# Seven of sixteen head pairs transposed by VectorE, nine by TensorE in place, the last queries of two pairs scored together, and the order of all instructions written out

## The chip, the cores and the metric

The kernel runs on one core of one Trainium2 chip. The core has TensorE for matrix products, VectorE, ScalarE and GpSimd for work on elements, and SyncE, whose queue issues the DMAs. TensorE writes to PSUM, eight banks of 512 float32 columns on 128 partitions; everything else lies in SBUF or, behind the DMAs, in HBM. The metric is the time of one execution in microseconds, the median of the runs shown. In the profile TensorE's products stand as PE, its weight loads as PEld, VectorE as DVE, ScalarE as ACT, GpSimd as POOL.

## What is computed

```python
B, H, S, D = 4, 8, 576, 64
q_rot, k_rot = rotate(q), rotate(k)          # x1*cos - x2*sin, x1*sin + x2*cos
scores = matmul(q_rot, k_rot^T) / sqrt(D)
attn = exp(scores - max(scores))
attn = attn / (sum(attn) + 1e-9)
x = (attn @ v), heads side by side           # 4 x 576 tokens of 512
xn = (x - mean) / sqrt(var + 1e-6) * g_ln
out = x + relu(xn @ w_ch1) @ w_ch2           # 512 -> 2048 -> 512
```

All of it is float32 in and out. The MLP's weights come as 64-bit words that the kernel decodes itself, and each is split into a high and a low part in TensorE's float32r format, so that one product takes three passes (high x high, high x low, low x high).

## The kernel before

The 32 heads are worked in 16 pairs (index i); a pair's two heads j share the 128 partitions, 64 each. `attention(i)` goes over the 576 queries in five groups c: four of 128 queries, each giving two units (one per head) of 128 queries by 576 keys, and a last group of 64 queries, in which both heads fill one unit. A unit lies in two PSUM banks. `scores` (L425, products in L432 and L436) writes it; VectorE takes the maximum of each row (L477); ScalarE takes the exponential and the sum (L489). The result p has queries on the partitions, while the product with v needs keys there, so TensorE transposes p, 128 x 128 at a time (L533), with smaller steps for the tail of the keys (L553) and for the last queries (L572, L573), into PSUM, and VectorE or ScalarE copies it out (`copy`, L285). The product with v is made in two parts of 256 and 320 queries: one product over the keys left over (L621) and sixteen records over the others (L625), two heads side by side in 64 columns each. The sums get an epsilon (L499, L501), are inverted (L505), transposed by TensorE to a row (L591), copied, written to memory and read back spread over the partitions, and the scaling (L635) writes x.

Before that, `prepare(i)` loads queries and keys and turns them by the rotary angles: three elementwise steps each for keys and queries, 6 a pair, 90 for pairs 1 to 15 (L403, L405), on GpSimd but for pair 1, where VectorE may take them.

Beside attention run `decode` and `weight_sums`: every weight tile is put together from its bits by ScalarE, VectorE and GpSimd (L765 to L794), stored to memory, and combined into sums of quarters (L840 to L850) that the second stage uses. The tokens lie in five blocks. `layer_norm(n)` normalizes one: means by a TensorE product (L669), squares by ScalarE (L698), their mean by four groups of products in 32 columns each (L685), and the spread of the inverse (L714). Block 0 goes through the MLP beside attention (`mlp_unit`, L889, 32 units of twelve products). Blocks 1 to 4 go in two pairs (`pair_inputs`, `pair_stage`, L1042), each pair by a scheme with seven products in place of eight: 2 pairs x 8 stages x 7 units of twelve products.

The order of all work comes from `Plan.run`. Every step is a task with the engines that it may run on and an assumed duration on each, what it comes after, which buffers of which ring it takes and gives back (`RINGS`), and a priority. The planner goes through time, starts the first task that can start, on the engine that is free first, and records it; the instructions of each engine are then chained in that order. `reorder` shifts the priorities by drawn amounts (`ORDER`). Score units take slots of two banks ("sc", three); transpositions and products with v take single banks ("t", two). After the first layer norm the third score slot becomes two single banks ("m"), which the MLP and the layer norms use.

```python
tt = add({"PE": 0.47}, tr, [exps[2 * c + j]], N + 0.1 * j, take=[ring_t(i, j)], ...)
...
parts[a].append(add(how_c, cp_, deps, N + 0.1 * j, take=take, give=[ring_t(i, j)], ...))
...
how2 = {"POOL": 1.43, "DVE": 0.76} if i < 2 else {"POOL": 1.43}
```

Of the kernel before, what the change touches and what calls it, by code (L numbers as in the profile page):

```python
# [10 lines left out]
F32 = mybir.dt.float32  # L11
# [9 lines left out]
P = 128  # L21
S = 576
# [14 lines left out]
PARTS = slice(0, 2 * P), slice(2 * P, S)  # L37
# [17 lines left out]
TM = 99  # L55
RATE = 285.0
EARLY = 30.0
AFTER = 0.0
SLACK = 0.7
XPRIO = 1e4  # L60
XB = 0.0
WARM = 16
HOLD = {28: (14, 2), 29: (15, 0), 30: (15, 2), 31: (15, 4)}
ORDERED = True
ORDER = [
# [5 lines left out]
]  # L71
SIZES = 0.5, 2.0, 5.0, 12.0, 30.0
SHARE = 0.08, 0.01, 0.1, 0.3, 0.3
# [4 lines left out]
def mixed(x):  # L78
    for m in (0x7FEB352D, 0x846CA68B):
        x = ((x ^ x >> (16 if m == 0x7FEB352D else 15)) * m) & 0xFFFFFFFF  # L80
    return x ^ x >> 16


def chance(seed, i):
    return mixed((mixed(seed) + i * 0x9E3779B9) & 0xFFFFFFFF) / 2.0**32


def reorder(tasks):
    kinds = {}
    kind = [kinds.setdefault(t.fn.__code__, len(kinds)) for t in tasks]  # L90
    n = len(tasks)
    for seed in ORDER:
        m = mixed(seed)
        size, mode, later = SIZES[m % 5], m // 5 % 5, m // 25 % 5 == 0
        lo = int(chance(seed, 7) * n) if mode == 3 else 0
        for i in range(lo, min(lo + 60, n) if mode == 3 else n):
            t = tasks[i]
            if later and "SP" not in t.how:
                continue
            k = kind[i] + 1000003 if mode in (0, 4) else i  # L100
            if chance(seed, 2 * k + 100) < SHARE[mode]:
                d = size * (2 * chance(seed, 2 * k + 101) - 1)
                if later:
                    t.release += d
                else:
                    t.prio += d


class Task:
    def __init__(self, how, fn, after, prio, take, give, lag, release, name, behind, port, over, of, which):  # L110
# [3 lines left out]
        self.start = self.end = None  # L114


class Plan:
# [32 lines left out]
    def run(self):  # L150
        free = dict.fromkeys(("PE", "DVE", "ACT", "POOL", "SP", "NONE"), 0.0)
        slots = {k: [(0.0, j) for j in range(n)] for k, n in RINGS.items()}
        channel = port = 0.0
        reorder(self.tasks)
        waiting = sorted(self.tasks, key=lambda t: t.prio)
        now = 0.0
        while waiting:
            later = []
            started = False
            for t in waiting:  # L160
                at = t.release
                for a in t.after:
                    if a.end is None:
                        at = None
                        break
                    at = max(at, a.end + (0.0 if t.how.keys() == {a.engine} != {"SP"} else a.lag))
                if at is None or any(a.start is None for a in t.behind):
                    continue
                picked = []
                for k, r in enumerate(t.take):  # L170
                    fit = [x for x in slots[r] if t.which is None or x[1] == t.which][t.take[:k].count(r) :][:1]
                    if not fit:
                        at = None
                        break
# [1091 lines left out]
```

## Time and profile before

| | us |
|---|---|
| median of three runs | 693.29 |
| lowest, highest | 692.33, 695.5 |
| span of the profiled execution, first to last instruction | 690.1 |
| PE busy | 670.6 |
| DVE busy | 515.5 |
| POOL busy | 417.3 |
| ACT busy | 376.0 |

For the profiled execution only its span is recorded; the median of the runs lies 3.2 us above it. Busy times count overlapping records once. Matmuls overlap in the array, so the duration of one record is longer than the distance to the next; the distance is read from the chain of waits, where a group of records stands with the time by which it moved the chain on.

### The profile page before, as it was taken

What the parts mean: (1) busy time and instruction counts of PE and PEld (TensorE: products, weight loads), DVE (VectorE), ACT (ScalarE), POOL (GpSimd) and SP (SyncE); (2) the same over time, 40 slices, a digit from 0 to 9 for tenths busy, and PEclk for the clock granted to TensorE, in tenths of its full rate; (3) what the DMA queues carried; (4) which work ended last, traced back from release to release, by engine and by line L of the source; (5) the groups of instructions that cost most, each with busy time, mean ns of one, the idle gap of its engine ahead of it and who ended that gap; (6) DMA issues with size and microseconds to landing.
All of it is one profiled execution on the core that took longest, in us unless ns stands there. A gap on an engine that the chain in (4) does not pass through costs nothing.

```text
span 690.1 us, 11545 instructions
## 1 busy us (share of the span) xinstructions
PE 670.6 (97%) x3954; PEld 506.5 (73%) x3954; DVE 515.5 (75%) x856; ACT 376.0 (54%) x805; POOL 417.3 (60%) x318
## 2 busy tenths in 40 slices
PE   6889999999999999999999999999999999999997
PEld 5555555667656667666666669989999999999996
DVE  4789888778877777778776759885877768757574
ACT  2678779667669676687666644341434243414130
POOL 4668866657769498787793614761457727515153
PEclk8899999999999999999999999999999999999999
DMA  8455664455947766568575347759678886666663
GB/s 270 138 175 179 238 215 158 152 180 168 318 164 249 249 236 217 194 228 302 193 245 191 118 153 242 219 186 307 213 214 262 270 269 206 221 217 214 211 217 133
DMA packets 85323, 147.20 MB, mean 213 GB/s; under 512 B 10880, under 2 KB 56592, under 8 KB 85264
## 3 DMA queue, kind: packets, MB, share of 16 engines
q1 hardware_dynamic: 84128, 145.60, 64.2%
q10 hardware_dynamic: 1136, 0.85, 0.4%
q8 instruction: 32, 0.52, 0.3%
q14 instruction: 27, 0.22, 0.1%
HBM read 108.60 MB, written 37.82 MB: 212 GB/s over the span
## 4 chain that ended last, share of the span: by engine, by line
PE 88%; ACT 5%; DVE 4%; DMA 1%; issue 1%; ACTq 0%; DVEq 0%
PE n L1042 40%; PE m L889 12%; PE sc L436 10%; PE t L625 9%; PE t L533 8%; PE sc L432 2%; PE t L621 2%; PE t L572 1%; ACT p L489 1%; PE t L553 1%; ACT pt L285 1%; DVE mx L477 1%; PE m L685 1%; DVE ws L850 1%; PE t L591 1%
## 5 line engine op out<-in xcount | busy, mean ns | idle before, releaser
L1042 PE MATMUL n<-x,w 128*128 128x448 f32 x672 | 140.1, 367 | 0.0
L1042 PEld LDWEIGHTS n<-x,w 128*128 128x128 f32 x672 | 125.5, 188 | 12.2 <-issue 1.1
L477 DVE TENSOR_REDUCE mx<-sc 128x1 f32<-128x576 f32 x144 | 104.5, 749 | 31.9 <-PE sc L436 24.7
L489 ACT ACTIVATE p<-sc,mx 128x576 f32<-128x576 f32 x144 | 106.0, 740 | 28.6 <-DVE mx L477 24.0
L1042 PE MATMUL n<-o,w 128*128 128x448 f32 x576 | 121.0, 368 | 0.0
L1042 PEld LDWEIGHTS n<-o,w 128*128 128x128 f32 x576 | 107.8, 188 | 10.9 <-issue 0.5
L969 ACT ACTIVATE o<-tmp 128x448 fp32r<-128x448 f32 x96 | 55.2, 579 | 104.8 <-PE n L1042 39.0
L976 POOL TENSOR_TENSOR o<-tmp,o 128x448 fp32r<-128x448 f32 x53 | 66.2, 1268 | 44.0 <-ACT o L969 43.2
L436 PE MATMUL sc<-xk,xq 64*128 64x288 f32 x512 | 85.2, 438 | 2.8 <-DVE xq L345 1.5
L533 PE MATMUL t<-ident,p 128*128 128x128 f32 x512 | 78.3, 285 | 7.0 <-DVE pt L285 1.9
L533 PEld LDWEIGHTS t<-ident,p 128*128 128x128 f32 x512 | 57.0, 143 | 37.9 <-issue 12.6
L285 ACT COPY pt<-t 128x512 f32<-128x512 f32 (+1 forms) x99 | 54.3, 551 | 53.8 <-PE t L533 46.6
L774 POOL TENSOR_TENSOR fw<-fw,w 128x512 int32<-128x512 int32 x32 | 43.3, 1358 | 44.0 <-ACT w L768 20.3
L625 PE MATMUL t<-pt,v 128*64 128x320 f32 (+1 forms) x512 | 69.1, 412 | 0.0
L436 PEld LDWEIGHTS sc<-xk,xq 64*128 64x128 f32 x512 | 48.2, 190 | 23.9 <-issue 10.8
L1114 DVE TENSOR_TENSOR xt<-xt,n 128x448 f32<-128x448 f32 x80 | 48.6, 615 | 18.9 <-PE n L1042 18.6
L625 PEld LDWEIGHTS t<-pt,v 128*64 128x64 f32 x512 | 33.9, 136 | 31.3 <-issue 12.3
L889 PE MATMUL m<-xh,w 128*128 128x512 f32 x128 | 47.9, 417 | 0.0
L889 PE MATMUL m<-hh,w 128*128 128x512 f32 x128 | 47.6, 415 | 0.0
L1101 POOL TENSOR_TENSOR tmp<-tmp 128x448 f32<-128x448 f32 x15 | 20.3, 1356 | 44.9 <-DVE tmp L1080 39.7
L405 POOL TENSOR_TENSOR xs<-xs,rope_sb 128x576 f32<-128x576 f32 x30 | 45.5, 1522 | 1.1 <-DMA xs<-in_qk 1.1
L285 DVE COPY pt<-t 128x512 f32<-128x512 f32 (+1 forms) x61 | 37.0, 613 | 10.2 <-PE t L533 6.6
(119 smaller groups left out, 1146.4 us busy)
## 6 DMA issues: line engine op xcount, KB each, us to landing
w<-s SPq DMA_DIRECT2D x64, 512.0 KB
w<-v SPq DMA_DIRECT2D x96, 256.0 KB
s<-ws SPq DMA_DIRECT2D x32, 512.0 KB
xs<-in_qk SPq DMA_DIRECT2D x30, 288.0 KB
w<-in_w1p SPq DMA_DIRECT2D x16, 512.0 KB
v<-w SPq DMA_DIRECT2D x16, 512.0 KB
w<-in_w2p SPq DMA_DIRECT2D x16, 512.0 KB
v<-in_vp SPq DMA_DIRECT2D x16, 320.0 KB
```

The costliest lines, as they stand in the source:

```text
L285: (ACT.copy if plan.engine == "ACT" else DVE.tensor_copy)(o, i)
L405: eng().tensor_tensor(out=x[step], in0=x[step], in1=rope_sb[:, step], op=ALU.mult)
L436: PE.matmul(ps[:, a, :HS], lhsT=q[r, c * P : (c + 1) * P], rhs=k[r, KEYS[a]], start=True, stop=True)
L477: DVE.tensor_reduce(out=mx, in_=st["ps", i, n][:, :, :HS], axis=AX.XY, op=ALU.max, negate=True)
L489: ACT.activation(out=halves(p), in_=st.pop(("ps", i, n))[:, :, :HS], func=AF.Exp, bias=st.pop(("mx", i, n)), scale=1.0, accum_out=total)
L533: PE.transpose(ps[:, k], p[:, j, j * T + k * P : j * T + (k + 1) * P], ident)
L625: PE.matmul(ps[r], lhsT=v[:, k, r], rhs=pt[:, j, k], start=False, stop=k == 3)
L889: PE.matmul(ps, lhsT=wt, rhs=x, start=c + m == 0, stop=c + m == NC + 1)
L969: ACT.activation(out=o[0], in_=x(), func=AF.Relu if relu else AF.Copy)
L976: eng().tensor_tensor(out=lo, in0=x(), in1=raw(hi), op=ALU.subtract)
L1042: PE.matmul(ps, lhsT=wt, rhs=x, start=fresh and kc + z == 0, stop=kc + z == 3, skip_group_check=True)
L1114: DVE.tensor_tensor(out=o, in0=o, in1=ps(which, h), op=ALU.add)
```

## The change

Of the 16 pairs, seven (4, 6, 8, 10, 12, 13, 15; those not in `TURNED`) have their exponentials transposed by VectorE, in place, in blocks of 32 x 32 (`turn`). Their product with v then runs over blocks of 32 keys: v lies in four shifted copies on the four groups of 32 partitions (four loads instead of one), and `pv` issues 18 x 4 x 2 products with 32 rows, 64 columns and 128 or 160 moving columns into four banks. The nine others are transposed by TensorE as before, but ScalarE alone copies the result back over the exponentials (`cross`, `back`), and their product takes all 576 queries at once, as 512 and 64 columns (`pv_crossed`).

The last 64 queries of pairs i and i + 1 (i even) are scored in one step of eight products (`tail_scores`), one tile for each pair. The sums of a pair lie in one tile; ScalarE adds the epsilon, VectorE inverts and transposes them, and they go through memory once a pair. In `layer_norm` of blocks 1 to 4 the four squares are added up by GpSimd or VectorE (`merge`), and TensorE takes one group of products instead of four. All PSUM is four slots of two banks, used by everything. The sums of the last two of eight weight groups are put off into the second stage (`late_sums`); the decoded weights go through memory for that. In `pair_inputs` the loads and steps are put in another order. The rings change: w from 6 to 4, v, inv and ws from 2 to 1, sq from 1 to 3. Every rotation step may now run on VectorE.

`reorder` no longer shifts priorities: a table of two characters a task (`PLACES`) gives each task its place, another (`SIDES`) its engine, 0 for the first named and 1 for the second, and `Plan.run` takes each engine's tasks in just that order.

```diff
-RINGS = {"sc": 3, "t": 2, "m": 2, "p": 3, "p9": 1, "pt0": 1, "pt1": 1, "x": 2, "xs": 3, "v": 2, "inv": 2, "w64": 2, "fw": 2, "w": 6, "h": 4, "xn": 1, "ln": 1, "sq": 1, "xt": 5, "n": 0, "o": 0, "tmp": 0, "ws": 2}
+RINGS = {"sc": 4, "m": 0, "pt": 2, "x": 2, "xs": 3, "v": 1, "inv": 1, "w64": 2, "fw": 2, "w": 4, "h": 4, "xn": 1, "ln": 1, "sq": 3, "xt": 5, "n": 0, "o": 0, "tmp": 0, "ws": 1, "lf": 0, "ls": 0}
-LATE = {"n": 6, "o": 13, "tmp": 9}
+LATE = {"n": 6, "o": 13, "tmp": 9, "lf": 1, "ls": 1}
+DEFERRED = 6
...
+TURNED = (0, 1, 2, 3, 5, 7, 9, 11, 14)
+ROPES = 16
+SUMMED = (1, 2, 3, 4)
...
+PLACES = (
...
+SIDES = (
...
+    places = "".join(PLACES)
+    for t, hi, lo in zip(tasks, places[::2], places[1::2], strict=True):
+        t.prio = len(CODE) * CODE.index(hi) + CODE.index(lo)
+    for t, side in zip(tasks, "".join(SIDES), strict=True):
+        t.side = list(t.how)[int(side)]
...
-            ld = add({"SP": 576 / RATE}, load, [], p - 8, behind=[ev["l_q"]], take=["x" + nm, "xs"], name=f"load{i}{nm}")
+            ld = add({"SP": 576 / RATE}, load, [], p - 8, behind=[ev["loaded"]] + ([ev["s", (i - 2, 4 - i % 2)]] if i > 1 else []), take=["x" + nm, "xs"], name=f"load{i}{nm}")
+            ev["loaded"] = ld
...
+            if i in TURNED:
+                SP.dma_start(v[:, 0], vp[divmod(i, NPB)].rearrange("p n d -> p (n d)"))
+                return
+            src = vp[divmod(i, NPB)].rearrange("(a k) n d -> k a (n d)", a=4)
+            for a in range(4):
+                SP.dma_start(v[a * BLK : (a + 1) * BLK], src)
+
+        ev["v", i] = add({"SP": 1.0 if i in TURNED else 6.2}, load, [], nominal(i, 0) - 4, behind=[ev["l_q"]], take=["v"], name=f"v{i}")
...
+    def tail_of(i, j):
+        d = j ^ i & 1
+        return slice(d * T, (d + 1) * T)
+
+    def tail_scores(i, tiles):
+
+        for a in range(2):
+            for j in range(2):
+                for n, ps in enumerate(tiles):
+                    k, q = st["k", i + n], st["q", i + n]
+                    r = slice(j * D, (j + 1) * D)
+                    PE.matmul(ps[tail_of(n, j), a, :HS], lhsT=q[r, S - T :], rhs=k[r, KEYS[a]], start=True, stop=True)
 
...
+        def turn(c):
+            p = st["pt", i][:, 4] if c == 4 else st["pt", i][:, c::5]
+            DVE.transpose(p, p)
...
+            two = st["turn", i, c] = banks[plan.task.got["sc"][0]]
+            p = flat()
+            if c < 4:
+                for j in range(2):
+                    for k in range(4):
+                        at = (2 * c + j) * S + j * T + k * P
+                        PE.transpose(two[:, j, k * P : (k + 1) * P], p[:, at : at + P], ident)
+                return
...
+        def invert():
+            t = totals[i % 2]
+            DVE.reciprocal(t[:, :9], t[:, :9])
+            st["row", i] = smp.tile([P, BLK], F32, name="row", bufs=2)
+            DVE.transpose(st["row", i], t)
...
+            if part == 0:
+                for go in both(slice(0, P), v[:, 0, 4 * P :], (S - T, S - T), True, False):
+                    go()
+            for k in ((0,), (1, 2), (3,))[part]:
+                halves_ = [both(slice(j * D, (j + 1) * D), v[:, 0, k * P + j * D :][:, :D], (j * (S + T) + k * P, (4 * j + k) * T), False, k == 3) for j in range(2)]
+                for pair in zip(*halves_):
+                    for go in pair:
+                        go()
...
+            for b in range(18 * part // PARTS, 18 * (part + 1) // PARTS):
+                for a in range(4):
+                    r = slice(a * BLK, (a + 1) * BLK)
+                    for j in range(2):
+                        k, of = divmod((b - 2 * j) % 18, 4)
+                        own = a // 2 == j ^ i & 1
+                        u0, u1 = (0, 4 + own) if j == 0 else (5 - own, 9)
+                        x0 = BLK if j == 0 or not own else 0
+                        if k == 4 and j:
+                            of += 2
+                        PE.matmul(
+                            tiles[a // 2][j * D : (j + 1) * D, a % 2, x0 : x0 + (u1 - u0) * BLK],
+                            lhsT=v[r, of, k * P + j * D : k * P + (j + 1) * D],
+                            rhs=pt[r, u0:u1, b * BLK : (b + 1) * BLK], start=b == 0, stop=b == 17)
...
+        def merge(c):
+            eng().tensor_tensor(out=z["sq", 0], in0=z["sq", 0], in1=z["sq", c], op=ALU.add)
...
+            if summed and c:
+                s = add(two, lambda c=c: merge(c), [s, v], N + 0.1 * c, give=["sq"], port=True)
+            if not summed or c == NC - 1:
+                v = add({"PE": 0.43}, lambda c=c: variance(c), [s], N, behind=[v] if c and not summed else [], give=["sq"], lag=0.2)
+            else:
+                v = s
...
+        if b < DEFERRED:
+            read, ev["sums", (y, g)] = make_sums(y, g, lambda: st["fw", b].bitcast(F32), l, prio, wsp, "ws", {"POOL": 1.3, "DVE": 0.68})
+            add({"NONE": 0.0}, lambda: None, read, prio, give=["fw"])
+            return
+        t = add({"SP": 1024 / RATE}, lambda: SP.dma_start(whole_w[y, g], st["fw", b].bitcast(F32)), [ev["d2", k] for k in range(k0, k0 + NC)], prio)
+        add({"NONE": 0.0}, lambda: None, l + [t], prio, give=["fw"])
+        ev["whole", (y, g)] = t
```

## Rows read from the trace of the kernel before

**Rows 1.** Busy time by stretch: stretch, length, busy PE, PEld, DVE, ACT, POOL (records), clock, DMA share, GB/s.

```profile
11.80:404.30 392.50, 381.93 (x2489) 246.25 (x2490) 305.81 (x521) 277.49 (x628) 283.02 (x207) 0.99 0.61 207
404.30:690.10 285.80, 281.89 (x1427) 254.60 (x1425) 203.55 (x315) 96.15 (x173) 131.68 (x104) 1.00 0.70 221
```

**Rows 2.** The page's strips over 40 slices: granted TensorE clock in tenths, and DMA rate.

```profile
PEclk8899999999999999999999999999999999999999
...
GB/s 270 138 175 179 238 215 158 152 180 168 318 164 249 249 236 217 194 228 302 193 245 191 118 153 242 219 186 307 213 214 262 270 269 206 221 217 214 211 217 133
```

**Rows 3.** The chain of waits, 140 to 182 us: start, step, engine, tile, line, records.

```profile
142.06 0.20 PE t L591
142.26 1.17 PE sc L436 x8
143.43 1.02 PE t L533 x8
...
145.86 0.22 PE t L553 x2
...
149.67 0.43 PE t L621 x2
150.10 1.88 PE t L625 x16
...
153.58 1.12 PE sc L432 x8
...
160.11 0.51 PE t L572 x8
160.62 0.06 PE t L573
...
164.45 2.77 PE m L889 x12
...
172.45 0.54 PE t L621 x2
172.99 2.33 PE t L625 x16
```

**Rows 4.** The chain of waits, 400 to 470 us.

```profile
406.77 0.33 PE m L685 x8
...
416.20 0.88 PE m L714 x8
417.08 29.27 PE n L1042 x144
446.35 0.75 PE m L669 x2
```

**Rows 5.** Groups by form: line, engine, operation, shapes, count, busy, mean ns, idle before.

```profile
L405 POOL TENSOR_TENSOR xs<-xs,rope_sb 128x576 f32<-128x576 f32 x30 | 45.5, 1522 | 1.1 <-DMA xs<-in_qk 1.1
...
L432 PE MATMUL sc<-xk,xq 64*64 64x288 f32 x128 | 19.0, 415 | 0.1
...
L850 DVE TENSOR_TENSOR ws<-fw,ws 128x512 fp32r<-128x512 f32 x12 | 14.9, 1239 | 2.7 <-ACT ws L847 2.6
...
L692 DVE TENSOR_TENSOR xc<-xt,m 128x448 f32<-128x448 f32 x16 | 9.0, 615 | 1.5 <-PE m L669 1.4
...
L692 DVE TENSOR_TENSOR xc<-xt,m 128x512 f32<-128x512 f32 x4 | 2.5, 682 | 0.6 <-PE m L669 0.6
...
L405 DVE TENSOR_TENSOR xk<-xk,rope_sb 128x576 f32<-128x576 f32 x1 | 0.8, 829 | 0.4 <-DMA xk<-in_qk 0.4
```

**Rows 6.** Busy time of L285 (DVE, ACT), then of L501 (DVE), 11.8 to 404.3 us.

```profile
11.80:404.30 392.50, 50.36 (x108) 66.32 (x148) 0.99 0.61 207
...
11.80:404.30 392.50, 15.89 (x21) 0.99 0.61 207
```

**Rows 7.** VectorE's instructions in order of time, 176 to 200 us.

```profile
175.81 1.58 DVE L850 TENSOR_TENSOR ws<-fw,ws 128x512 fp32r<-128x512 f32 x1
...
179.25 0.68 DVE L840 TENSOR_TENSOR fw<-fw 128x512 f32<-128x512 f32 x1
```

More of the change, by code (lines that the diff above doesn't have):

```diff
@@ L74 @@
 OVER = {"PE": 0.0, "DVE": 0.08, "ACT": 0.1, "POOL": 0.045, "NONE": 0.0}
 PORT = {"DVE": 0.13, "POOL": 0.05}
[L78 to L85, printed above, removed]
-def reorder(tasks):
[L89 to L106, printed above, removed]
+CODE = "ABCDEFGHIJKLMNOPQRSTUVWXYZabcdefghijklmnopqrstuvwxyz0123456789!#$%&()*+,-./:;<=>?@[]^_{|}~"
@@ L214, in run @@
-        self.length = max(t.end for t in self.tasks)
+        queues, ready, followers, missing, earliest = {e: [] for e in engines}, [], {}, {}, {}
+        for t in sorted(self.tasks, key=lambda t: t.prio):
+            missing[t], earliest[t] = len(t.after) + len(t.behind), 0.0
+            for a in [*t.after, *t.behind]:
+                followers.setdefault(a, []).append(t)
+            if t.side != "NONE":
+                queues[t.side].append(t)
+        ready = [t for t in self.tasks if t.side == "NONE" and not missing[t]]
@@ new lines, in begin @@
+        def begin(t):
+            at, picked = earliest[t], []
+            for k, r in enumerate(t.take):
+                fit = [x for x in slots[r] if t.which is None or x[1] == t.which][t.take[:k].count(r) :][:1]
+                if not fit:
+                    return None
+                picked.append((r, fit[0]))
+                at = max(at, fit[0][0])
+            if t.side == "SP" and at > 0:
+                at += SLACK
+            if t.side != "NONE":
+                at = max(at, free[t.side], port if self.shared(t, t.side) else 0.0)
+            return at, picked
@@ new lines, in attention, with part @@
+        N = nominal(i, 8) + 5
+        crossed = i in TURNED
+        count = 3 if crossed else PARTS
+        slots = ["sc"] if crossed else ["sc", "sc"]
+        for k in range(count):
+            def part(k=k):
+                (pv_crossed if crossed else pv)(k)
+            first, end = k == 0, k == count - 1
+            t = add({"PE": (2.13, 2.13, 1.1)[k] if crossed else 0.13 + 5.25 / PARTS}, part, turned + [ev["v", i]] if first else [t], N, behind=[ev["pv"]] if first and i else [], take=slots if first else [], give=["pt", "v"] if end else [], lag=0.2 if end else 0.1, name=f"pv{i}" if first else "")
+            if first:
+                t0 = t
@@ new lines, in pair_inputs, with op @@
+        there = [ev["late1"]] if q == 0 else []
+        last = {0: [], 1: []}
+        def op(i, c, s, after):
+            t = operand((q, 0, c, i), at(c, s), after + there + ([ev["late"]] if i == 4 else []), prio, f"x{c}{i}")
+            last[c].append(t)
+            return t
+        l1 = [op(1, c, 0, [l[c, 0]]) for c in range(2)]
+        l3 = [op(3, c, 3, [l[c, 3]]) for c in range(2)]
+        t1 = [add(two, diff(at(c, 0), at(c, 2), at(c, 0)), [l1[c], l[c, 2]], prio, port=True) for c in range(2)]
@@ L1018, in pair_stage @@
+        for c in range(2):
+            op(4, c, 1, [t4[c]])
+        ev["x made"] = add({"NONE": 0.0}, lambda: None, last[0] + last[1], prio, give=["ln"] + 3 * ["sq"])
     def pair_stage(q, m, y, g, k0, a, b):
@@ L1191, in rope_attention_then_ln_mlp @@
             weight_sums(k // NC % 2, k // (2 * NC))
+    add({"NONE": 0.0}, lambda: None, attn, 0.0, take=["sc"], which=RINGS["sc"] - 1, give=["m"])
     work = [t for t in plan.tasks if t not in attn]
```

673 lines of the change are left out of this document (350 added, 323 removed), and 5 rows, old and new, of the table ORDER.

## The prediction

> **What bounds the kernel now.** I read the busy time by stretch first [rows 1]. The span of 690.1 us has two stages: attention with the decoding of the weights and the first block's MLP, 11.8 to 404.3 us, and then the MLP of four blocks in two pairs, to the end. TensorE is busy 381.9 of 392.5 us in the first and 281.9 of 285.8 in the second, at a granted clock of 0.99 and 1.00, which is the upper level, 2.4 GHz; the page's strip has nine tenths or more from the third of its 40 slices on [rows 2]. VectorE is busy 305.8 of 392.5 (78%), GpSimd 283.0 (72%), ScalarE 277.5 (71%). So TensorE is the bound and VectorE the next.
>
> Busy time flatters TensorE, because records overlap. What a group really takes is its step in the chain of waits [rows 3]: 1.17 us for the scores of 128 queries, 1.12 for those of the last 64, 1.02 for eight transpositions, 0.22 for the two of a tail, 0.51 + 0.06 for the ten small ones, 0.20 for the row of sums, 0.43 + 1.88 and 0.54 + 2.33 for the two products with v, 2.77 for an MLP unit. A head pair's transpositions take 4 x 1.02 + 2 x 0.22 + 0.57 = 5.09, its products 5.18. Over the first stage: 63 x 1.17 = 73.7 (one stands before 11.8), 16 x 1.12 = 17.9, 16 x 5.09 = 81.4, 32 x 0.20 = 6.4, 16 x 5.18 = 82.9, 32 x 2.77 = 88.6, and three layer norms of 0.75 + 4 x 0.33 + 0.88 = 2.95 [rows 4], 8.9: 359.8 in all. 392.5 - 359.8 = 32.7 us is stall.
>
> **The change part by part, on TensorE.** Last queries together: 16 steps of 1.12 become 8, each with eight products in the four corners of the array. If four corners run as the two now do, a step stays 1.12; if only two do, it is 2.24 and nothing is won. The eight records of today last 415 ns each and fit in 1.12 because they overlap [rows 3, 5]; I take 1.2, hence 9.6 for 17.9: -8.3 (0 at worst).
>
> Seven pairs turned on VectorE lose their transpositions: 7 x 5.09 = -35.6. The nine others keep the same 32 + 4 + 10 transpositions: 0. The rows of sums, 32 x 0.20, go to VectorE: -6.4.
>
> Products with v: VectorE turns only 32 x 32 blocks, so a turned pair multiplies 32 keys at a time: 18 blocks x 4 row groups x 2 heads = 144 products, 288 records, meant to run eight at once. The columns alone: 160 at two cycles per column and record (a 448-column record steps 29.27/144 = 203 ns [rows 4], 448 x 2/2.4 = 187), 133 ns, x 36 slots = 4.8 us. No row shows 32-row tiles. A slot of today's 64-column products costs 1.88/8 - 0.213 = 0.022 over its columns; a slot of the scores, in two row groups, 1.17/4 - 0.240 = 0.052 [rows 3]. That makes 5.6 or 6.7; I take 6.1, between them, since this form is tiled both ways: 7 x (6.1 - 5.18) = +6.4. The far bounds are 4.8 and, if only two tiles overlap as in the rows, 144 x 0.155 = 22. The nine others take 512 and 64 columns instead of 256 and 320: the same columns in the same 20 slots, with 64-column slots of 0.06, the step of the smallest transposition [rows 3], 5.3: 9 x 0.1 = +1 (0 to +4).
>
> Squares summed off TensorE: three of four steps of 0.33 in four blocks, -2.0 in each stage.
>
> First stage: -8.3 - 35.6 - 6.4 + 6.4 + 1 - 2.0 = -44.9. Second: -2.0.
>
> **On VectorE.** It loses its PSUM copies, 50.4 us [rows 6], all to ScalarE or gone, and the 21 additions of epsilon, 15.9 [rows 6], which at 0.76 each for four or five columns are mostly waiting. It gains: 48 of the 90 rotation steps (counted in the diff's side table, where a 1 is VectorE; two are there now), 46 x 0.83 = 38.2 [rows 5]; the turns, 28 of 1152 columns and 7 of 576. No row has a turn. Two subtractions give 0.615 us at 448 columns and 0.682 at 512, so 1.05 ns per column [rows 5]: 1.35 and 0.75, 43.1 in all; at twice that rate they would be 22, at half of it 86. Smaller: scaling in two row patterns and one inversion per pair +4, half of seven merges of squares +2, two weight operations less -2. 305.8 - 50.4 - 15.9 + 38.2 + 43.1 + 4 = 324.8. GpSimd loses 46 rotation steps of 1.52 [rows 5], 70, and the weight sums put off, some 20: about 193. ScalarE takes all copies of the nine pairs, 9/16 of 50.4 + 66.3, 66, for the 66.3 it has now [rows 6]: unchanged.
>
> So TensorE's demand is 359.8 - 44.9 = 314.9 and VectorE's 324.8. Were the stall the same 32.7, the stage would take 347.6, with VectorE 93% busy instead of 78%. VectorE stands in every unit's loop (maximum, then exponential), and four PSUM slots now serve scores, transpositions, products and MLP alike, so stalls grow; I add 5 us. The floor is VectorE's 324.8 with some 10 of starting and last waits, 335.
>
> **On the queues.** Every engine's order is fixed by the tables, as it was fixed before by the planner; behind a late head instruction its whole engine waits. New such heads: a turned pair's first product waits for all five turns, with the next scores and MLP units queued behind it on TensorE; the scaling of a pair waits for one trip of all nine sums through memory where it was two, and holds two of the four PSUM slots meanwhile. Both are in the 5 us. SP gains four loads of v in place of one for seven pairs, 7 x 3 x 0.33 MB, and 1 MB out and in for two weight groups: 11 MB on 147, 243 GB/s over a shorter run, where one slice of today reaches 318 [rows 2]. v and its scales have one buffer, so a pair's v starts after the products of the pair before; 20 us to the next products cover it. Weight buffers fall from six to four: in the second stage a unit takes 12 x 0.203 = 2.44 us, so a load has three units, 7.3 us, instead of 12; half a megabyte at 221 GB/s [rows 1] needs 2.4. The late weight sums lie on GpSimd, busy 131.7 of 285.8 there [rows 1]: costed at nothing, and a stage is kept waiting if that cover fails.
>
> **Sum.** The profiled execution spans 690.1; the median, 693.3, lies 3.2 above it, which I keep. First stage 352.5 instead of 392.5, second 2 less: 693.3 - 40 - 2 = 651.
>
> **Rivals.** (1) VectorE becomes the bound through GpSimd. Beside a GpSimd operation the same 512-column step takes 1.58 us, alone 0.68, and twelve of them average 1.24 [rows 5, 7]. If 48 rotations and 30 weight operations each lose 0.4, VectorE needs 356; with 20 of waits the stage takes 376, the whole 675; if the 35 turns lose 0.5 too, 692. For it: VectorE's waits stand in the order of its queue. Against: GpSimd's own load falls by a third. The Trainium skill (SBUF — State Buffer, Who interferes with whom) says that a VectorE instruction with at most one SBUF input, outside the two-port modes, does not contend with GpSimd; a turn is of that kind, which speaks against 692. No row here shows a turn.
>
> (2) Records start one at a time at a pace of their own. Needed are 133/8 = 17 ns per record. The nearest row, eight small products of the variance in four column groups, takes 0.33 us, 41 ns each, the change to and from other products included [rows 4]. At 41 a pair's products take 11.8, 7 x 5.7 = 40 more: 691, no change. The Trainium skill (TensorE: Matmul & The Clock Gate, Part 1) puts the least distance of two starts at about 25 ns however small the product; by that 288 records take 7.2, and the sum is 659.
>
> (3) The other side: the eight tiles don't run together but two by two, as all that the rows show. Then 22 a pair, 7 x 15.9 = 111 more, 762. It decides from 12.1 us per pair on, where 7 x 6.0 eats the 42 gained. Against: products of one pair of tiles already cost one slot, and small records step at 0.06 in a row [rows 3], below 0.155.
>
> (4) The second stage starves: four weight buffers, late sums on the same queue. If 20 units lose 0.7 us each, 14: 665.
>
> **How the numbers follow.** Forecast 651, own range 637 (stall at VectorE's floor) to 664 (stalls 18 more, or products at 7.2): 0.62. Rival 1 0.17, mostly near 675. Rival 2 at 41 ns 0.06. Rival 3 0.06. Rival 4 0.09. The range of 8 in 10 takes forecast and rivals 1 and 4 but for the ends: 636 to 679. What can be told from no change is 0.5%, 3.5 us. Faster: 0.62 + 0.16 + 0.09 = 0.87; same: half of rival 2 and the end of rival 1, 0.05; slower 0.08.
>
> **What would show it.** First stage near 352 us, TensorE's second stage near 284; turns of 1.35; products of a turned pair near 6.1 as a step of the chain (rival 3: 22, rival 2: 12); a tail step near 1.2; VectorE over 90% busy in the first stage, its two-input steps under 0.9 us (rival 1: over 1.1); TensorE without idle time in the second (rival 4: idle before weight loads). The prediction is wrong if products or turns cost twice as taken, or if the fixed order stalls TensorE over 50 us.

## The result, and the profile after

The kernel takes 674.95 us (median of four runs, 673.14 to 679.14) where the kernel before takes 692.81 beside it: a ratio of 0.974, 95% interval 0.970 to 0.978. It is faster by 17.9 us; 42 were forecast. The sign was right and 675 lies in the range, but more than half of the gain did not come. The profiled execution spans 673.5 us.

The windows of the two stages, columns as in [rows 1] (length, busy time of PE, PEld, DVE, ACT and POOL with their counts, granted clock, DMA share, GB/s):

```profile
11.80:383.80 372.00, 340.52 (x3849) 231.05 (x3849) 301.94 (x482) 255.14 (x539) 185.81 (x135) 0.97 0.70 226
383.80:673.50 289.70, 285.01 (x1380) 256.39 (x1380) 235.40 (x378) 100.89 (x193) 117.93 (x88) 0.99 0.76 247
```

The first stage lost 20.5 us (392.5 to 372.0; forecast 352.5), the second grew by 3.9 (285.8 to 289.7; forecast 283.8). These two misses, 19.5 and 5.9, are the whole difference but for 1.4 us: the time of the profiled execution lies 1.8 us above its span here, and 3.2 were kept.

The strips of the granted clock and of the transfers after, against [rows 2], and the engines' shares of the chain of waits, before and after:

```profile
PEclk8999999999999999998999899999999999999999
GB/s 257 167 242 202 216 204 133 152 241 266 215 251 297 229 302 268 216 270 291 211 182 229 200 228 278 309 286 254 322 267 209 264 265 219 218 217 211 211 210 198
```
```profile
PE 88%; ACT 5%; DVE 4%; DMA 1%; issue 1%; ACTq 0%; DVEq 0%
```
```profile
PE 61%; DVE 16%; DMA 10%; ACT 7%; issue 4%; SPq 1%; POOL 0%; DVEq 0%; POOLq 0%; ACTq 0%
```

Before, the chain that ended last was TensorE's own work. After, TensorE holds 61% of it, VectorE, ScalarE and landings of DMAs a third.

**The steps that were costed.** First a piece of the chain after (start, length, what; it answers to [rows 3]), then the last half of one turned pair's products in the timeline of TensorE, then groups of VectorE by form (count, busy time, mean ns of one, idle time before):

```profile
347.03 1.13 PE sc L488 x16
```
```profile
376.94 2.70 PE L669 MATMUL sc<-pt,v 32*64 32x128 f32 x144
```
```profile
L557 DVE STREAM_TRANSPOSE pt<-pt 128x1152 f32<-128x1152 f32 x28 | 37.9, 1361 | 2.6 <-ACT pt L509 2.5
...
L959 DVE TENSOR_TENSOR ws<-fw,ws 128x512 fp32r<-128x512 f32 x10 | 8.8, 880 | 0.4 <-ACT ws L956 0.3
...
L557 DVE STREAM_TRANSPOSE pt<-pt 128x576 f32<-128x576 f32 x7 | 5.3, 757 | 0.0
```

Tails of two pairs step at 1.13 (1.2 taken), a turned pair's 288 records at 2 x 2.70 = 5.4 (6.1 taken; from the first start to the last these 144 take 2.41, so 5.4 is rather high), the crossed pairs' products at 5.27 (5.3), turns at 1.36 and 0.76 (1.35 and 0.75). With 63 x 1.17 for the other scores, 9 x 5.09 for transpositions, 88.6 for the MLP and 2.95 + 2 x 1.96 for the layer norms (block 0 keeps its four groups of squares), TensorE's demand is 73.7 + 9.0 + 45.8 + 47.4 + 37.8 + 88.6 + 6.9 = 309.2 us; the forecast had 314.9. So what is left of 372.0 is 62.8 us of stall. It was 32.7 before, and 37.7 forecast; over 50 was named as a sign that the prediction is wrong.

**Where the stall shows.** TensorE's granted clock over four stretches after, and over the whole of before:

```profile
48.00:54.00 6.00, 5.32 (x29) 3.73 (x30) 3.13 (x6) 5.11 (x12) 3.01 (x3) 0.72 0.76 269
232.00:238.00 6.00, 5.64 (x25) 3.97 (x26) 4.24 (x11) 3.44 (x9) 3.35 (x3) 0.72 0.95 308
314.00:323.00 9.00, 7.78 (x186) 6.61 (x190) 6.21 (x8) 6.61 (x11) 7.86 (x6) 0.62 0.67 240
383.00:391.00 8.00, 7.23 (x19) 5.43 (x20) 7.61 (x15) 6.40 (x14) 0.20 (x1) 0.57 0.84 307
```
```profile
11.80:22.00 10.20, 9.20 (x33) 6.11 (x33) 4.58 (x9) 6.07 (x14) 6.14 (x6) 0.53 0.45 175
22.00:690.00 668.00, 654.62 (x3881) 494.73 (x3881) 504.78 (x828) 367.57 (x788) 408.56 (x306) 1.00 0.65 213
```

Before, the clock is at 1.2 GHz once, at the start. After, it is there four times more. In the third the lost share is (1 - 0.62) x 9.0 = 3.4 us of TensorE's work, in the four together 1.7 + 1.7 + 3.4 + 3.4 = 10.2 (an estimate, as if TensorE had worked all through). Ahead of each TensorE had waited, in the timeline of its steps:

```profile
48.68 0.84 PE L580 MATMUL sc<-ident,pt 64*128 64x64 f32 x10 [2.83 <-ACT pt L509]
...
232.30 1.66 PE L569 MATMUL sc<-ident,pt 128*128 128x128 f32 x8 [3.02 <-ACT pt L509]
...
313.31 1.24 PE L475 MATMUL sc<-xk,xq 64*128 64x288 f32 x8 [1.42 <-DVE hl L1022]
...
383.77 0.74 PE L1168 MATMUL n<-x,w 128*128 128x448 f32 x1 [4.13 <-ACT x L1076]
```

Not every such wait was followed by the lower clock: 2.16 us ahead of the scores at 295.25 were not (1.00 from 290 to 312).

The last of the four is the second stage's first product. By the estimate 3.4 of the 3.9 us by which this stage grew are its slow clock, but that is not shown: with half of the turns left out (below) the first eight microseconds of the stage have a clock of 0.79, and it takes the same 289.7. Another piece of the chain shows what can stand behind a wait:

```profile
174.66 0.68 DVE ws L959
...
175.53 6.04 DMA s<-ws
181.57 0.02 issue
181.60 0.02 ACT ws L956
181.62 0.50 issue
182.12 1.01 ACT pt L587
183.14 0.04 issue
183.18 1.97 PE sc L475 x8
```

ScalarE's next cast (L956) needs the one buffer for weight sums, which a store gives back when it has landed, 6.04 us later; the copy L587, queued behind it, frees the PSUM slot that the scores at 183.18 want. No run gives this buffer its second place back.

From the records I paired every step that takes a PSUM slot with the instruction after which it is given back, and summed the time between. The columns are three kernels, two of them experiments below:

| us of slots held in the first stage | after | no maximum | all left out |
|---|---|---|---|
| scores until their exponentials | 611 | 489 | 447 |
| products with v, until scaled | 245 | 242 | 230 |
| MLP units | 178 | 168 | 162 |
| transpositions | 155 | 141 | 136 |
| layer norms, start | 55 | 54 | 51 |
| sum, of four slots over the stage | 1244 of 1488, 84% | 1094 of 1422, 77% | 1026 of 1375, 75% |
| of these a score unit of 128 queries, mean | 4.26 | 3.37 | 3.09 |

Paired in the same way, the kernel before holds its eight banks for 60% of the first stage, where the kernel after holds them for 84%. Its score unit of 128 queries stays nearly as long, 4.05 us. What grew is the rest: transpositions, products with v, MLP and layer norms held 744 us of single banks before and hold 633 us of slots, 1266 us of banks, after, since each now takes slots of two banks (an MLP unit writes only one of its two).

Summing each TensorE step's distance to the next over that of its quickest fifth, TensorE loses 68 us in the first stage after, and 30 of them lie ahead of steps that take a slot, mostly until an exponential has ended. Some 10 of the 30 lie ahead of transpositions, which also read exponentials. Set against the time at which each step's data were there, the slot alone was what came last for 23 us. With all left out the two sums are 43, and 10. In the kernel before they are some 55, and 16. So by this count TensorE loses some 13 us more than before, about all of it ahead of steps that take banks, where the count by prices of the chain gives 62.8 - 32.7 = 30. How large the growth is depends on how a step is priced; either way it is more than the 5 us forecast.

### The profile page after: what moved, and what is told of

It is laid out like the page before. It is cut to its first block, busy times and chain, and to the rows that moved or that the text cites. A ratio compares the mean times of both kernels' runs of the same rounds, so it can differ in the third digit from the quotient of the medians.

```text
span 673.5 us, 13928 instructions
## 1 busy us (share of the span) xinstructions
PE 632.4 (94%) x5268; PEld 493.2 (73%) x5268; DVE 543.1 (81%) x880; ACT 358.3 (53%) x734; POOL 306.2 (45%) x230
## 4 chain that ended last, share of the span: by engine, by line
PE 61%; DVE 16%; DMA 10%; ACT 7%; issue 4%; SPq 1%; POOL 0%; DVEq 0%; POOLq 0%; ACTq 0%
PE n L1168 37%; PE sc L995 7%; PE sc L475 6%; PE sc L643 4%; DVE mx L502 4%; ACT pt L509 3%; PE sc L669 3%; DMA w<-in_w2p 3%; DVE pt L557 2%; DMA s<-ws 2%; PE sc L569 2%; ACT pt L587 1%; DVE xc L779 1%; DMA v<-in_vp 1%; DMA xs<-in_qk 1%
## 5 line engine op out<-in xcount | busy, mean ns | idle before, releaser
L509 ACT ACTIVATE pt<-sc,mx 128x576 f32<-128x576 f32 x144 | 105.9, 740 | 58.9 <-DVE mx L502 57.3
L1083 POOL TENSOR_TENSOR o<-tmp,o 128x448 fp32r<-128x448 f32 x30 | 40.5, 1361 | 74.8 <-ACT o L1076 74.8
L643 PE MATMUL sc<-pt,v 128*64 128x512 f32 (+2 forms) x324 | 50.4, 417 | 1.0 <-DMA v<-in_vp 0.9
L669 PE MATMUL sc<-pt,v 32*64 32x160 f32 (+1 forms) x2016 | 43.1, 305 | 3.0 <-issue 1.4
L995 PE MATMUL sc<-xh,w 128*128 128x512 f32 x128 | 45.3, 412 | 0.5 <-ACT pt L509 0.3
L569 PE MATMUL sc<-ident,pt 128*128 128x128 f32 x288 | 39.6, 284 | 6.0 <-ACT pt L509 4.9
L557 DVE STREAM_TRANSPOSE pt<-pt 128x1152 f32<-128x1152 f32 (+1 forms) x35 | 43.0, 1240 | 2.6 <-ACT pt L509 2.5
L995 PE MATMUL sc<-hh,w 128*128 128x512 f32 x128 | 44.1, 404 | 0.2 <-ACT pt L509 0.2
L669 PEld LDWEIGHTS sc<-pt,v 32*64 32x64 f32 x2016 | 36.8, 136 | 8.8 <-issue 5.9
L569 PEld LDWEIGHTS sc<-ident,pt 128*128 128x128 f32 x288 | 32.2, 144 | 14.3 <-ACT pt L509 9.2
L885 POOL TENSOR_TENSOR w<-fw,w 128x512 fp32r<-128x512 f32 x22 | 29.7, 1354 | 24.5 <-ACT w L881 24.5
```

The source lines that it names most:

```text
L509: ACT.activation(out=halves(p), in_=st.pop(("ps", i, n))[:, :, :HS], func=AF.Exp, bias=st.pop(("mx", i, n)), scale=1.0, accum_out=total)
L557: DVE.transpose(p, p)
L569: PE.transpose(two[:, j, k * P : (k + 1) * P], p[:, at : at + P], ident)
L643: yield lambda o=o, x=x: PE.matmul(o, lhsT=w, rhs=x, start=start, stop=stop)
L669: PE.matmul(tiles[a // 2][j * D : (j + 1) * D, a % 2, x0 : x0 + (u1 - u0) * BLK], lhsT=v[r, of, k * P + j * D : k * P + (j + 1) * D], rhs= ...
L995: PE.matmul(ps, lhsT=wt, rhs=x, start=c + m == 0, stop=c + m == NC + 1)
```

## The experiments

The theories: (0) TensorE's work still paces the first stage. (2) VectorE's work does. (1) The fixed order waits for landings of transfers, for little else. (4) The lower clock is the cost. (5) TensorE waits for one of the four PSUM slots, and these are held by chains through VectorE, ScalarE and landings that are nearly equally long, so that none of them paces alone. All runs change the kernel after. Gains are differences of the ratios to before, times 693 us; two ratios tell 3.5 us or so apart. The expectations quote gains as differences of medians, which are up to 1.5 us less or more. The last column is of the one profiled execution, whose time can lie some us off the median (4.5 below it without the maximum, 4.0 below with all left out, 3.0 above without stores).

| run | median | ratio, 95% | gain on after | first stage |
|---|---|---|---|---|
| after | 674.95 | 0.974 (0.970 to 0.978) | | 372.0 |
| half of the turned products | 670.42 | 0.968 (0.964 to 0.972) | 4.5 | 366.3 |
| half of the turns | 671.95 | 0.969 (0.967 to 0.972) | 3.3 | 368.6 |
| no stores | 663.52 | 0.956 (0.952 to 0.959) | 12.9 | 360.8 |
| v in a buffer of its own | 675.68 | 0.973 (0.970 to 0.977) | 0.7 | 369.6 |
| half of the maximum | 668.62 | 0.965 (0.960 to 0.970) | 6.2 | 361.9 |
| identity products in the gaps | 683.68 | 0.986 (0.982 to 0.990) | -8.2 | 380.5 |
| few loads | 660.95 | 0.954 (0.951 to 0.956) | 14.3 | 359.2 |
| no stores, few loads | 659.73 | 0.952 (0.948 to 0.956) | 15.5 | 357.1 |
| no maximum | 665.14 | 0.961 (0.956 to 0.965) | 9.3 | 355.6 |
| all left out | 650.07 | 0.937 (0.932 to 0.941) | 26.0 | 343.7 |
| third weight buffer | 674.64 | 0.974 (0.971 to 0.978) | 0.0 | 371.3 |
| third buffer, half maximum | 666.41 | 0.960 (0.957 to 0.963) | 9.6 | 363.7 |

**Half of the turned products.**

```diff
-            for b in range(18 * part // PARTS, 18 * (part + 1) // PARTS):
+            for b in range(9 * part // PARTS, 9 * (part + 1) // PARTS):
...
-  start=b == 0, stop=b == 17)
+  start=b == 0, stop=b == 8)
```

> Leaves out the products over half of the keys (9 of 18 key blocks) of the seven turned pairs, so its output is that of half the keys there; all else, the order of every engine and every transfer stand. It takes 7 x 2.7 = 18.9 us of work off TensorE in the first stage. Theory 1 (the stall stands for landings of transfers and for places of the fixed order, not for TensorE's work): the kernel gains at most 6 us on 675. Theory 0 (TensorE's work still paces the first stage): it gains 15 or more. Theory 2 (VectorE paces it): at most 5.

4.5 us of 18.9 came back. Theory 0 falls: TensorE's work is no longer what the stage waits for.

**Half of the turns.**

```diff
         def turn(c):
             p = st["pt", i][:, 4] if c == 4 else st["pt", i][:, c::5]
+            p = p if c == 4 else p[:, 0]
             DVE.transpose(p, p)
```

> VectorE turns only one of the two units of each of the 28 turns of 1152 columns, so half of the turned weights of the seven pairs are not written; all else stands. It takes 28 x (1.36 - 0.76) = 16.8 us of work off VectorE in the first stage. Theory 2 (VectorE, slowed by GpSimd or not, paces the first stage): the kernel gains 12 or more on 675. Theory 1 (landings and places of the fixed order pace it): at most 6. Theory 0 (TensorE's work paces it): about 0 to 3.

3.3 of 16.8, which the runs can't tell from zero; 12 or more is out. Theory 2 falls in its plain form: work of VectorE outside the loop of the scores counts for little, by the middle of the interval a fifth.

**No stores.**

```diff
-            SP.dma_start(split_w[u][:, :, r], ...)
+            if u == UNITS[0]:
+                SP.dma_start(split_w[u][:, :, r], ...)
...
-  lambda i=i, n=n: SP.dma_start(sums_w[y, g, i], raw(z[n]))
+  lambda i=i, n=n: SP.dma_start(sums_w[y, g, i], raw(z[n])) if (y, g) in ((0, 0), (0, 3), (1, 3)) else None
```

> Only the first unit's decoded split weights and only the weight sums of one first-stage group are stored; the loads behind them read these again, as many bytes as before, so the MLP is computed with the wrong weights in part. 51 stores of half a megabyte or less, some 21 MB of the 158, leave the first stage; the work of TensorE, VectorE, ScalarE and GpSimd and its order stand. Theory 1 (the first stage waits for landings that its stores crowd and for buffers that a store must give back): it gains 10 or more on 675, most of it in the first stage. Theories 0 and 2 (an engine's own work paces it): at most 4.

12.9 us, as theory 1 expected, and the first stage alone is 11.2 us shorter (360.8 for 372.0): stores, which add no work to any of the four engines, cost more than either engine's 17 to 19 us of work.

**A buffer for v.**

```diff
-"v": 1,
+"v": 1, "vc": 1,
...
+                v = st["v", i] = vcpool.tile([P, 1, 5 * P], F32, name="vc")
```

> The whole computation; the crossed pairs' v gets a buffer of its own of 2.5 KB a partition, so that v of a turned pair no longer waits for the products of the crossed pair before it, and the other way round; order and work of every engine stand. Theory 1 (each late head costs its own few microseconds): the waits on v in the chain go (8.25 us of landing before the last pair among them), the kernel gains 3 to 8 on 675. Theories 0 and 2: 0 to 2.

Nothing to be told from zero; theory 1 expected 3 to 8. The chain before the last pair's products, with the buffer free:

```profile
352.24 3.06 DMA sums<-row
...
358.92 0.43 SPq L1115
...
361.92 8.81 DMA v<-in_vp
```

The load still goes out at 362 (after: 364): it stands in SP's fixed order behind the trip of the row of sums and what follows it. Here a free buffer moved nothing, as the place in the queue decided.

**Half of the maximum.**

```diff
-  DVE.tensor_reduce(out=mx, in_=st["ps", i, n][:, :, :HS], ...)
+  DVE.tensor_reduce(out=mx, in_=st["ps", i, n][:, :1, :HS], ...)
```

> VectorE takes the maximum of each of the 144 units over half of its keys (288 of 576 columns, one of the two banks), so exponentials are taken against another maximum; all else stands. It takes about 144 x 0.33 = 47 us off VectorE, all of it between scores and exponential, in the loop that holds the four PSUM slots. Theory 2 (VectorE's work or its place in the slot loop paces the first stage): it gains 20 or more on 675. Theory 1 (landings and places of the fixed order): at most 8, as half of the turns gave 3.0 for 16.8. Theory 5 (no part paces alone, and each engine's work counts by about a fifth, as 3.0 of 16.8 on VectorE and 4.5 of 18.9 on TensorE): 8 to 11.

6.2 us. VectorE loses 33 us of busy time (301.9 to 269.0), not 47: the reductions lose 42 (747 to 448 ns each in the median), while steps of the decoding take some 10 longer. A fifth of the 33 comes back. It was below theory 5's 8 to 11, in theory 1's range of at most 8, and far from theory 2's 20.

**Identity products in the gaps.**

```diff
+    def hold(ps, n):
+        for _ in range(n):
+            PE.matmul(ps, lhsT=ident, rhs=ident, start=True, stop=True)
...
+        hold(tiles[0][:, 0, :P], 6 if (i, c) == (13, 1) else 0)
```

> The whole computation and, beside it, 52 products of the identity with itself, 128x128, put on TensorE just ahead of five steps that it waits for in the profile after (12 before the step at 48.7 us, 12 before 232.3, 6 each before 313.3 and 316.1, 16 before the second stage's first product at 383.8), written where that step then writes. Theory 4 (the granted clock, at its lower level for 20 us of the span behind these gaps, costs half of that): those stretches stay at the upper level and the kernel gains 4 to 9 on 675. The others: it gains at most 2 and may lose as much, since the dummy products stand ahead of work.

8.2 us lost where theory 4 expected 4 to 9 gained. (The second of the five groups stood, by mistake, at another step of the same pair, at 218 us.) The timeline of TensorE tells why; L471 are the added products, in brackets the idle time ahead of them:

```profile
49.19 4.39 PE L471 MATMUL sc<-ident 128*128 128x128 f32 x24 [2.23 <-ACT pt L514]
...
218.05 2.94 PE L471 MATMUL sc<-ident 128*128 128x128 f32 x24 [0.18 <-ACT pt L514]
...
320.77 1.60 PE L471 MATMUL sc<-ident 128*128 128x128 f32 x12 [1.41 <-DVE hl L1029]
...
388.76 3.81 PE L471 MATMUL n<-ident 128*128 128x128 f32 x32 [1.53 <-DVE xt L702]
```

A product of the identity with itself needs nothing but a place to write. At 49.19, 320.77 and 388.76 it waited all the same, 2.23, 1.41 and 1.53 us: there the place in PSUM alone was enough to keep TensorE waiting. This the run shows directly, though it was made for something else. In the kernel after, the step at 48.68 had its data from 27.5 us on and its slot from 48.5, the scores at 313.31 from 301.7 and 313.3; the second stage's first product lacked data too, since in this run its operands were made only after 391.

As they couldn't run in the gaps, the added products, 52 in all, stood behind them, ahead of work, and took some 14 us. The clock, in the same columns as above:

```profile
48.00:54.00 6.00, 4.82 (x33) 4.59 (x34) 2.34 (x4) 3.25 (x8) 1.40 (x1) 0.72 0.90 300
239.00:245.00 6.00, 5.34 (x26) 3.35 (x26) 3.59 (x10) 3.94 (x9) 4.03 (x4) 0.72 0.92 300
314.00:323.00 9.00, 7.35 (x40) 4.80 (x40) 7.60 (x14) 7.08 (x18) 6.04 (x5) 1.00 1.05 276
323.00:332.00 9.00, 8.73 (x315) 7.43 (x312) 7.13 (x9) 5.75 (x9) 7.08 (x6) 1.00 0.47 167
392.00:402.00 10.00, 7.85 (x31) 6.34 (x30) 9.89 (x17) 6.56 (x14) 1.77 (x1) 0.83 0.63 225
```

It fell as before behind the first group, and at 239, where the misplaced group was missing. The third stretch stayed at the upper level, and in the fourth the loss is half, (1 - 0.83) x 10.0 = 1.7 us; a new one of 3.4 us stands at 105. What the clock alone costs is not settled by it: the added work hides it.

**Few loads, and no traffic.**

```diff
-            z["x"] = w64p.tile([P, NC, 2 * P], U32, name="w64")
-            SP.dma_start(z["x"], ...)
+            if k < 2:
+                st["w64", k] = w64p.tile([P, NC, 2 * P], U32, name="w64")
+                SP.dma_start(st["w64", k], ...)
+            z["x"] = st["w64", k % 2]
```

> Of the 32 loads of a packed weight unit (512 KB each) only the first two are made; the other units decode what is left in these two buffers, so the MLP's weights are wrong from the third unit on. 15.7 MB and 30 landings leave the first stage, all engines' work and order stand. Theory 1: as with the stores left out (11.4 for 21 MB), 8 or more gained, and the steps of ScalarE that wait for these landings in the chain (5.5 us each at 41.5, 214.6, 222.6, 271.2) go. Theory 5: about a sixth of the 49 us that 15.7 MB take at 320 GB/s, 8. Theories 0 and 2: at most 4.

> Both at once: the stores left out as in the run without stores, and the 30 loads of packed weights left out, 37 MB in all, so the MLP is computed with wrong weights. Theory 1 (the fixed order waits for landings, and little else): it gains 20 or more on 675, the first stage comes near 350 us. Theory 5 (the rest of the stall lies in the loop of scores, maximum, exponential and the four PSUM slots, which no transfer touches): 12 to 18 gained, and stall of 40 us or more is left.

14.3 without the loads, and no landing of packed weights is left in the chain, as expected; 15.5 without loads and stores. The two don't add (12.9 + 14.3 = 27.2), so they must cover one another; by which waits was not traced. Theory 1 as "and little else" falls, and theory 5's two numbers (12 to 18 gained, 40 or more of stall left) came true: with all transfers of the first stage down from 226 to 128 GB/s, 357.1 - 309.2 = 48 us of stall are left.

```profile
11.80:368.90 357.10, 336.10 (x3849) 228.67 (x3849) 299.35 (x482) 253.93 (x539) 186.76 (x135) 0.98 0.43 128
```

**No maximum, and all left out.** The second is the edits of no traffic, no maximum and no turn together.

```diff
-  mx = st["mx", i, n] = smp.tile([P, 1], F32, name="mx")
-  DVE.tensor_reduce(out=mx, ...)
+  pass
...
-  ACT.activation(..., bias=st.pop(("mx", i, n)), scale=1.0, accum_out=total)
+  ACT.activation(..., bias=0.0, scale=1.0, accum_out=total)
```

> No maximum is taken: the 144 reductions on VectorE are left out and the exponentials have a bias of zero (for these inputs the softmax comes out the same up to rounding). It takes 103 us off VectorE and, what matters to theory 5, shortens the time that scores hold their two PSUM slots, from 4.3 us on average by at least the 0.75 to 1.4 us of the reductions, some 130 to 180 of the 1244 slot-microseconds that the trace after shows held in the first stage (of 4 x 372). Theory 5 (what TensorE waits for is mostly a PSUM slot that an exponential gives back): it gains 12 or more on 675, and the waits of TensorE for exponentials fall by half. Theory 2 (VectorE's work): 20 or more. Theory 1 (landings): at most 8, as transfers keep their places.

> Left out together: the stores and loads of the run without traffic (37 MB), all maxima (103 us of VectorE) and all turns on VectorE (43 us), so only TensorE, ScalarE and GpSimd keep their work, and the attention of the turned pairs and the MLP are wrong. If the causes are separate and add up (15.2 for the traffic, 12 to 20 for the maxima, 3 to 6 for the turns), it gains 30 to 41 on 675. If they cover one another (each engine's chain is nearly as long as the next, theory 5), the gain beyond the traffic's 15.2 is more than the sum, and the first stage comes near TensorE's own 311 us plus the start, some 330: 40 to 50 gained. If something not yet named holds the stage (the order of TensorE's own steps, ScalarE), it gains under 28.

Without the maximum 9.3 us, below theory 5's 12 and below theory 2's 20. All together 26.0, under the 28 below which I had said that something unnamed holds the stage. The parts sum to 15.5 + 9.3 + 3 to 6 = 28 to 31 (the turns were left out alone only by half, so 3 to 6 is an estimate from 3.3), so within the noise they add up. That they cover one another, from which theory 5 had expected 40 to 50, falls. The window with all left out, and the waits of TensorE for exponentials ahead of scores (time, times), after, without the maximum and with all left out:

```profile
11.80:355.50 343.70, 328.17 (x3849) 225.35 (x3849) 190.39 (x303) 238.76 (x538) 191.44 (x135) 0.99 0.45 133
```
```profile
  ACT pt L509: 10.1, 20
```
```profile
  ACT pt L508: 5.3, 13
```
```profile
  ACT pt L508: 3.1, 9
```

These waits fall by half without the maximum, as theory 5 had expected, and the sum ahead of all steps that take a slot falls from 30 us to some 20 without traffic, some 19 without the maximum and 10 with all left out. So the maxima and the traffic each work on the waits for slots. That is what stands of theory 5; its sizes were met only without traffic and with the last pair of edits below.

What remains, 343.7 - 309.2 = 34 us (and up to 4 more, as the profiled execution was the quickest), is close to the 32.7 that the kernel before had; what makes it up was not looked for. That the extra 30 us come from the maxima, the turns and the traffic is not shown by this: the kernel before has the same 144 maxima and loads the same weights, and no run takes them out of it. How much is the slots by themselves and how much the chains that hold them stays open too: no run has the slots alone changed, none the fixed order. All eight banks belong to the four slots, so there is no fifth.

The Trainium skill (TensorEngine Tiling (Array Packing), Gotcha 1: PSUM Pressure) says that different row tiles can't access one bank at the same time. The tails don't agree: there two row groups write different partitions of one bank, and 16 records step in 1.13 us, where half as many at a time would take 2.24. Whether row groups that write the same partitions of a bank, as a turned pair's four would with fewer banks, can do so, no run shows; fewer banks for them were not run.

**A third weight buffer.**

```diff
-"xs": 3, ... "w64": 2,
+"xs": 2, ... "w64": 3,
```

> The whole computation: three buffers for packed weight units instead of two, and two instead of three for the swapped halves of q and k (memory for one more 4 KB buffer is not there otherwise). Every engine's order and work stand. Theory 5 (TensorE waits for slots, and slots are held among others because ScalarE, with the exponentials in its queue, waits for a landing of packed weights): with a third buffer such a load no longer waits for the decoding of the unit two before (21.0 us of SP's waits), and part of the 14.0 us that leaving the loads out gave comes back, 3 to 8 gained on 675, unless the swapped halves now come late, which costs up to the same. Theories 0 and 2: 0 to 2.

> The same three buffers and the maximum over half of the keys (the softmax is the same up to rounding for these inputs). If the two act separately, the gain is 6.3 plus what the three buffers give alone; theory 5 (both shorten the time that exponentials hold a slot, and chains of nearly the same length cover one another) expects at least the sum: 9 to 15 on 675.

Alone nothing (0.0 us; 3 to 8 expected), though SP's waits for a free buffer of packed weights (L847 for the decoding's last step) fall from 21.0 us to 1.4. Loads of q and k wait instead, now that there are two buffers for their swapped halves (18.0 us for L428 behind the tails, 12.4 after). The waits of SP's queue, total, times and longest:

```profile
SPq L428 <- PE sc L488: 18.0, 6, 9.8
...
SPq L847 <- DVE fw L868: 1.4, 2, 1.1
```

With half of the maximum 9.6 beside 6.2: in the expected 9 to 15, but a difference that the runs can't tell from none. It and the kernel without a maximum (665.14) compute the whole result and are faster than both kernels; a maximum over part of the keys is safe only where no score lies so far above it that the exponential overflows.

## Why the prediction was right in sign and wrong in size

**TensorE's terms** held: 5.7 us less demand than forecast (309.2 against 314.9), as the turned products took 5.4 and the tails 1.13. One reading behind them was wrong: 448 x 2/2.4 is 373, not 187, and that row's products are float32r and step at 0.45 ns a column, about one cycle. The two cycles of float32 follow from 1.88 and 2.33 us for 256 and 320 columns in eight slots [rows 3], 0.88 ns a column, so the 133 ns stand. Rivals 2 and 3 (records at 41 ns, tiles two by two) are out: 2.70 us for 144 records is 18.8 ns each on average (16.8 from start to start), with eight tiles to run at once, and many start 6 to 14 ns behind the one before. The Trainium skill's 25 ns between two starts (TensorE: Matmul & The Clock Gate, Part 1), by which a pair takes 7.2, doesn't hold for these tiles here; the measured 5.4 decides.

**VectorE's terms** that were summed held, with 43.2 us of turns; the 48 rotations took 44.3 where 40 were summed. It is busy 301.9, not 324.8. About half of that is that steps left as they were became cheaper beside a quieter GpSimd (POOL 185.8 for 283.0 [rows 1]): the step of 1239 ns [rows 5] now takes 880 (L959). The other half is that the new order has eleven such steps fewer on VectorE in this stage (5 for 8 of the additions ahead of layer norms, 10 for 12 of L959's), of which the prediction counted two. So rival 1 falls, and that its 675 was the time that came is luck: VectorE is 81% busy, and half of the turns give 3.3 us. The turns don't contend: the 28 large ones take 1361 ns on average and 1379 at most, and those with GpSimd at work beside them all the time (1321 to 1378) are no slower than those with none (1334 to 1378). The Trainium skill (SBUF — State Buffer, Who interferes with whom) has this of instructions with one SBUF input, and the trace agrees.

**The step that failed** is "Were the stall the same 32.7 ... I add 5 us". The mechanism stood there, in "VectorE stands in every unit's loop, and four PSUM slots now serve scores, transpositions, products and MLP alike, so stalls grow"; its size was a guess that no row carried. It measured 30 us by the prediction's own prices, some 13 by the quickest fifths. What I costed at nothing belongs to the same term: the single buffer for weight sums (6.04 us of landing on the chain), v behind the products of the pair before (8.25 us, once), the weights' traffic in a shorter stage (15.5 us with both left out, though what that would give in the kernel before is not known). What could have been counted is the load on the banks: 60% before, 84% after, more than VectorE's 81%, and in no list of mine. The runs show that TensorE waits for slots and that maxima and traffic lengthen these waits; how the 30 us divide among them, the clock and the fixed order stays open.

**The clock.** The prediction assumed 2.4 GHz throughout. Gaps of 1.4 to 4.1 us stood ahead of four stretches at 1.2, 10 us of work in all by the estimate, 7 of them in the first stage; part of what the runs without traffic gave may be that these gaps and stretches become fewer (in the first stage of all left out the clock is 0.99, after 0.97).

**The second stage** was forecast at -2.0 and came at +3.9: up to 3.4 of the 5.9 between are the slow clock behind its first product; the rest was not traced. Rival 4 (starving for weights) is out: TensorE is busy 285.0 of 289.7, and its one long wait inside the stage is for VectorE (time, times, longest):

```profile
PE n L1168 <- DVE tmp L1216: 0.9, 1, 0.9
```

The range, 636 to 679, held the time because it was stretched for rivals 1 and 4, neither of which came, which is luck too; the likeliest case's own range, 637 to 664, did not hold it.

## What to carry to other kernels

Taking work off the busiest engine pays in full only down to the next resource, and that may be a ring of buffers, not an engine: sum for each ring the time from its taking to its giving back, divide by ring size and stage, and set the share beside those of the engines (84% here). A step that needs one bank and takes a slot of two counts twice. Where a change moves work from one engine to another, halves buffers and fixes the order, the stall is a term of its own; an added wait is to be sized by the landing behind it (3.4 to 8.3 us in the chain here) times how often it can come last. An engine that waits for a place to write is told from one that waits for data by giving it a product that needs no data.

## What was not expected of the hardware

- 32 x 64 tiles, eight at once, step at 18.8 ns a record (144 in 2.70 us, the last start 2.41 us after the first), where eight small products of the variance stepped at 41 [rows 4].
- Two row groups of the tails write different partitions of one bank and still overlap: 16 records in 1.13 us, four of them started within 20 ns of one another.
- VectorE turns 32 x 32 blocks of float32 in place at (1361 - 757)/576 = 1.05 ns a column, the rate of its two-input steps [rows 5], and GpSimd at work beside it changes nothing (1379 ns at most).
- A store or load of half a megabyte landed 5.5 to 6.0 us after its issue in all six places where the chain waits for one, at a mean of 226 GB/s.
